# First V rows stored by the Pool queue, Wo issued right behind Wk, V rows of two segments loaded by the ACT queue, constants built first

## The chip, the cores and the metric

One core of a Trainium2 chip, bfloat16 data. The metric is the device time of one execution in microseconds (us); medians are of a kernel's runs. Engines: PE is the TensorE matmul, PEld its weight load, DVE VectorE, ACT ScalarE, POOL GpSimd, SP SyncE, which here only issues DMAs. All times "at x us" are counted from the first instruction of the profiled execution.

## The reference, cut to what matters

```python
def _A_ref(x, mem0, Wq, Wk, Wv, Wo, seg_len):     # x: 1 x 2048 x 512; 32 heads of 128; seg_len 32; 8 memory rows
    mem = mem0
    for s in range(64):
        h = concatenate([mem, x[:, 32*s : 32*s + 32]], axis=1)              # 40 rows
        q, k, v = (einsum('btd,dhe->bhte', h, W) for W in (Wq, Wk, Wv))
        p = softmax(where(mask, einsum('bhqe,bhke->bhqk', q, k) * scale, -1e9))
        o = einsum('bhte,hed->btd', einsum('bhqk,bhke->bhqe', p, v), Wo)
        mem = o[:, :8]                       # the next segment needs Wo of this one
        outs.append(o[:, 8:])
    return concatenate(outs, axis=1)
h  = x + _A_ref(layernorm(x), ...)
h2 = h + _B_ref(layernorm(h), ...)           # a gated MLP with a 2048 x 2048 spatial weight
```

The 64 segments form a chain: `mem` of one feeds the next, so no segment can start before the one ahead is through Wo.

## The kernel before

Wq, Wk, Wv and Wo stay in SBUF during the loop. Each is 4.19 MB and is loaded in four quarters of 1 MB. Before the loop the kernel computes the projections of the *extra rows* (8 rows of each segment) for the first "chunks" of 16 segments. V of such rows is scaled, written to DRAM (`vext_d`, eight stores of 128 KB for chunk 0, four for the first half of chunk 1) and read back in another layout as `Vx`, two loads of 32 KB for each segment.

```python
def vx_mm(ck, n, bank, only=None):                    # the matmuls are line L498 of the profile
    ...
def vx_evac(ck, n, bank, eng="act"):
    ...                                               # scale PSUM into t by ACT or DVE
    dst = vext_d[ck, n // 4, 2 * (n % 4):2 * (n % 4) + 2, :, :].rearrange("g p f -> p g f")
    sp(lambda e: e.dma_start(dst, t.rearrange("p (g f) -> p g f", g=2)), reads=tok, writes=[("vext", ck, n)])   # L514

def load_vx(s):
    i = s % CK
    for b in range(2):
        src = vext_d[s // CK, b, :, 8 * i:8 * i + 8, :].rearrange("g k (r e) -> g (k r) e", r=2)
        sp(lambda e, b=b, src=src: e.dma_start(Vx[:, s % NVX, b, :], src),                                       # L520
           reads=[("vext", s // CK, n) for n in range(4 * b, 4 * b + 4)], writes=[("Vx", s % NVX, b)])
```

The load phase, in program order. SP is one queue of instructions, and what stands behind a waiting one waits too: in the trace of this kernel SP reaches the first `Vx` load at 45.35 us, issues the second at 48.51, and issues the two quarters of Wo behind these loads at 50.39 and 50.89.

```python
for mi in (2, 1):                                     # Wv, then Wk (Wq was issued earlier)
    for hq in range(4):
        load_w(mi, hq)
def load_wo(hq):                                      # L822
    sp(lambda e, hq=hq: e.dma_start(w_o[:, 8 * hq:8 * hq + 8, :], wor[:, 8 * hq:8 * hq + 8, :]), writes=[("Wo", hq)])
    em.mark_const(("Wo", hq))
def start_group(mm, ev, *a):
    ...
    mm(*a, bk)
    ev(*a, bk, "act" if cnt % 2 == 0 else "dve")
def start_v(ck, n):
    start_group(vx_mm, vx_evac, ck, n)

for i in range(2, 8):                                 # Q of the extra rows
    for ck in range(2):
        start_group(qkx_mm, qkx_evac, ck, i)          # matmuls L463, evictions L473
    if i == 6:
        for j in range(4, 7):
            ln_stats(j)                               # row statistics, 2 of 4 steps by Pool
        late_consts()                                 # masks, ones, selectors: some 60 Pool instructions
for n in range(8):                                    # V of the extra rows, each followed by a store on SP
    ...
    start_v(0, n)
    if n % 2 == 1:
        start_v(1, n // 2)
    ...
    if n == 4:
        ...
        load_wo(0)
load_wo(1)
for j in range(2):
    load_vx(j)
for i in range(8, 16):                                # K of the extra rows, needs Wk
    start_group(qkx_mm, qkx_evac, 0, i)
    if i in (11, 13):
        load_wo(i // 2 - 3)
```

In a segment, PE runs the projections (L289, L290), S, PV (L664 with V, L670 with Vx; 666 and 672 after the change) and then Wo (L699; 701 after), with matmuls of later extra rows (L498) between.

```python
WOQ = ((0, 0), (2, 0), (0, 1), (2, 1), (1, 0), (3, 0), (1, 1), (3, 1))
def Wo(cbs, bank, d0, d1):
    for c, b in cbs:
        for g in range(4):
            h = 16 * b + 4 * c + g                    # quarter h // 8 of Wo
            pe(lambda e, ...: e.matmul(..., lhsT=cTh[:, i, 8:40], rhs=w_o[:, h, d0:d1], ...), reads=[("cT", c, b), ("Wo", h // 8)], ...)
```

Of the kernel before, what the change touches and what calls it, by code (L numbers as in the profile page):

```python
# [178 lines left out]
def fast_path(nc, st, keep, A_x, A_mem0, A_Wq, A_Wk, A_Wv, A_Wo, A_seg_len, B_w_in, B_w_sp, B_b_sp, B_w_out, out):  # L179
# [15 lines left out]
    CK = 16  # L195
# [9 lines left out]
    em = Emitter(n_dma_sems=40)  # L205

    def sb(name, shape, dt):
        return st.enter_context(nc.sbuf_tensor("f_" + name, shape, dt))
# [26 lines left out]
    NVX = 3  # L235
    Vx = sb("Vx", [128, NVX, 2, 128], BF)
# [41 lines left out]
    def PB(b):  # L278
        return ("ps", b)

    def sp(fn, **k):
        return em.add("sp", fn, dma=True, **k)

    def pe(fn, **k):
        return em.add("pe", fn, **k)
# [9 lines left out]
    def act(fn, **k):  # L295
        return em.add("act", fn, **k)

    def dve(fn, **k):
        return em.add("dve", fn, **k)

    def pool(fn, **k):
        return em.add("pool", fn, **k)
# [10 lines left out]
    def xbuf(j):  # L313
        return (xn[:, j, :], [("xn", j)]) if j < 2 else (part[:, j, :], [("part", j, 0), ("part", j, 1)])
# [33 lines left out]
    def late_consts():  # L348
        pool(lambda e: e.memset(ones[:], 0.0), writes=["ones"])
        pool(lambda e: e.memset(Sc[:], 0.0), writes=["Sc"])  # L350
        pool(lambda e: e.memset(mask[:], 0.0), writes=["mask"])
        for c in range(4):
            q = slice(32 * c, 32 * c + 32)
            pool(lambda e, q=q: e.memset(ones[q, q], 1.0), writes=["ones"])
            pool(lambda e, q=q: e.affine_select(out=G_sb[q, :], in_=onesrc[q, 0:M], pattern=[[-1, M]], compare_op=ALU.is_equal,
                                                fill=0.0, base=0, channel_multiplier=1), reads=["onesrc"], writes=["G"])
            pool(lambda e, q=q: e.affine_select(out=F_sb[q, :], in_=onesrc[q, 0:32], pattern=[[-1, 32]], compare_op=ALU.is_equal,
                                                fill=0.0, base=-M, channel_multiplier=1), reads=["onesrc"], writes=["F"])
            pool(lambda e, q=q: e.affine_select(
                out=Sc[q, :].rearrange("p (s r) -> p s r", r=32)[:, :, XM:32], in_=onesrc[q, 0:32].rearrange("p (s r) -> p s r", r=8),  # L360
                pattern=[[-8, 4], [-1, 8]], compare_op=ALU.is_equal, fill=0.0, base=0, channel_multiplier=1),
                reads=["onesrc"], writes=["Sc"])
            m1 = mask[q, 0:160].rearrange("p (g t) -> p g t", t=40)[:, :, 16:40]
            pool(lambda e, m1=m1: e.affine_select(out=m1, in_=m1, pattern=[[0, 4], [1, 24]], compare_op=ALU.is_ge,
                                                  fill=NEG, base=8, channel_multiplier=-1), reads=["mask"], writes=["mask"])
            pool(lambda e, q=q: e.memset(mask[q, 160:224], NEG), writes=["mask"])
            for k in range(8):
                m2 = mask[q, 160:224].rearrange("p (hp r t) -> p hp r t", hp=2, r=2)[:, :, :, k:16]
                pool(lambda e, m2=m2, k=k: e.affine_select(out=m2, in_=m2, pattern=[[-16, 2], [-1, 2], [0, 16 - k]],
                                                           compare_op=ALU.not_equal, fill=0.0, base=-2 * k, channel_multiplier=1),  # L370
                     reads=["mask"], writes=["mask"])
        pool(lambda e: e.tensor_copy(out=mask[:, 224:448], in_=mask[:, 0:224]), reads=["mask"], writes=["mask"])


    def ln_bn(j):
        t, tok = xbuf(j)
        k = j % 3
        dve(lambda e: e.bn_stats(out=st1[:, k, :], in_=t), reads=tok, writes=[("st1", k)])

    def ln_root(j):  # L380
        k = j % 3
        dve(lambda e: e.bn_aggr(out=mv1[:, k, :], in_=st1[:, k, :]), reads=[("st1", k)], writes=[("mv1", k)])
        act(lambda e: e.activation(out=rs1[:, k:k + 1], in_=mv1[:, k, 1:2], func=ACT.Ln, bias=EPS), reads=[("mv1", k)], writes=[("rs1", k)])
        act(lambda e: e.activation(out=rs1[:, k:k + 1], in_=rs1[:, k:k + 1], func=ACT.Exp, scale=-0.5), reads=[("rs1", k)], writes=[("rs1", k)])

    def ln_stats(j):
        k = j % 3
        ln_bn(j)
        dve(lambda e: e.bn_aggr(out=mv1[:, k, :], in_=st1[:, k, :]), reads=[("st1", k)], writes=[("mv1", k)])
        pool(lambda e: e.tensor_scalar(out=rs1[:, k:k + 1], in0=mv1[:, k, 1:2], scalar1=EPS, scalar2=None, op0=ALU.add),  # L390
             reads=[("mv1", k)], writes=[("rs1", k)])
        pool(lambda e: e.tensor_tensor(out=rs1[:, k:k + 1], in0=rs1[:, k:k + 1], in1=mhalf[:, 0:1], op=ALU.pow),
             reads=[("rs1", k), "mhalf"], writes=[("rs1", k)])

    def ln_apply(j):
        t, tok = xbuf(j)
        k = j % 3
        dve(lambda e: e.tensor_scalar(out=t, in0=t, scalar1=mv1[:, k, 0:1], scalar2=rs1[:, k:k + 1], op0=ALU.subtract, op1=ALU.mult),
            reads=tok + [("mv1", k), ("rs1", k)], writes=tok)
# [99 lines left out]
                                                       start=(dc == 0), stop=(dc == DC - 1), tile_position=(0, 32 * c)),  # L499
                   reads=[("hTe", ck % 3, dc // 2), ("W", 2, n // 2)], writes=[PB(bank)])  # L500

    def vx_evac(ck, n, bank, eng="act"):
        if ck == 1 and n < 4:
            t, tok = (hbuf, xo)[n // 2][:, n % 2, :], [(("h", "xo")[n // 2], n % 2)]
        elif ck == 0:
            t, tok = part[:, n, :], [("part", n, 0), ("part", n, 1)]
        else:
            t, tok = Vs[:, 0, :], [("Vs", 0)]
        if eng == "act":
            act(lambda e: e.activation(out=t, in_=ps[:, bank, :], func=ACT.Copy, scale=VSC), reads=[PB(bank)], writes=tok)  # L510
        else:
            dve(lambda e: e.tensor_scalar(out=t, in0=ps[:, bank, :], scalar1=VSC, scalar2=None, op0=ALU.mult), reads=[PB(bank)], writes=tok)
        dst = vext_d[ck, n // 4, 2 * (n % 4):2 * (n % 4) + 2, :, :].rearrange("g p f -> p g f")
        sp(lambda e: e.dma_start(dst, t.rearrange("p (g f) -> p g f", g=2)), reads=tok, writes=[("vext", ck, n)])  # L514

    def load_vx(s):
        i = s % CK
        for b in range(2):
            src = vext_d[s // CK, b, :, 8 * i:8 * i + 8, :].rearrange("g k (r e) -> g (k r) e", r=2)
            sp(lambda e, b=b, src=src: e.dma_start(Vx[:, s % NVX, b, :], src),  # L520
               reads=[("vext", s // CK, n) for n in range(4 * b, 4 * b + 4)], writes=[("Vx", s % NVX, b)])



# [270 lines left out]


    act(lambda e: e.preload_act_table_set("natural_log_exp_and_others"))
    for _ in range(44):
        pe(lambda e: e.matmul(ps[:, 1, 0:128], lhsT=onesrc[:, 0:128], rhs=onesrc[:, 0:128], start=True, stop=True), reads=["onesrc"], writes=[PB(1)])
    ln_bn(0)  # L800
# [20 lines left out]
# [3 lines that stand above are left out]
# [4 lines left out]
    def start_group(mm, ev, *a):  # L828
        cnt = scnt[0]
        scnt[0] += 1  # L830
        bk = ebank[cnt % 4]
        mm(*a, bk)
        ev(*a, bk, "act" if cnt % 2 == 0 else "dve")

    def start_v(ck, n):
        start_group(vx_mm, vx_evac, ck, n)

    for i in range(2, 8):
        for ck in range(2):
            start_group(qkx_mm, qkx_evac, ck, i)  # L840
        if i == 6:
            for j in range(4, 7):
                ln_stats(j)
            late_consts()
    for n in range(8):
        if n < 3:
            ln_apply(n + 4)
# [3 lines that stand above are left out]
        if n == 2:  # L851
            xT(4, 6)
            ring_copy(0, 6)
        if n == 3:
            xT(5, 7)
            ring_copy(1, 7)
        if n == 4:
            xT(6, 6)
            xe_copy(2, 6)
            mem0_transpose(7)  # L860
            load_wo(0)
    load_wo(1)
    for j in range(2):
        load_vx(j)
    for i in range(8, 16):
        start_group(qkx_mm, qkx_evac, 0, i)
        if i in (11, 13):
            load_wo(i // 2 - 3)


    gx = []
# [287 lines left out]
    for rb in range(RB):  # L1159
# [19 lines left out]
        if rb in (2, 3):  # L1179
            r, j, bank = RB - 4 + rb, (rb - 1) % 2, zbank()  # L1180
# [49 lines left out]
    for tb in range(NTB):  # L1230
        for fb in range(len(ACC) if tb == 0 else 0, FB):
            if tb == 0:
                bank = 5 + fb % 3
            else:
                bank = MB[mcnt % 3]
# [19 lines left out]
    for d0 in (0, 256):  # L1255
        bank = 7 if d0 else 5
# [766 lines left out]
```

## Time and profile before

| | before |
|---|---|
| median of 3 runs | 862.03 us (860.3 to 863.04) |
| profiled execution, granted clock | 860.6 us, 0.992 |
| segment 0 / 1 / 2 | 21.12 / 10.78 / 9.73 us |
| last quarter of Wk / of Wo landed | 40.35 / 60.34 us |

Start with the page: the busy shares, and the span in 40 slices of 21.5 us, where each digit is a tenth.

```profile
span 860.6 us, 45965 instructions
...
PE 837.9 (97%) x22497; PEld 440.7 (51%) x19432; DVE 513.7 (60%) x1318; ACT 471.1 (55%) x1361; POOL 165.2 (19%) x423
...
PE   8959999999999999999999999999999999999997
...
PEclk9979999999999999999999999999999999999999
...
GB/s 319 371 248 39 91 55 42 65 59 71 69 94 42 69 62 44 65 42 65 59 71 71 87 47 96 54 97 72 59 57 50 186 282 1 1 110 98 37 13 40
...
q8 instruction: 166, 2.72, 1.4%
...
PE 94%; DMA 2%; SPq 1%; DVE 1%; ACT 1%; issue 1%
```

PE is busy 97% of the span, so only a few per cent can be won at all. The digit that stands out is slice 3 (43 to 65 us): PE 5, its clock 7. The rest of the span is full. (The line for q8 is needed later: 2.72 MB in 166 packets is 16 KB each.)

The stretches of the first three segments, with busy time and number of instructions of each engine, the clock, the DMA share and the rate:

```profile
core 0: us, PE busy (x) PEld busy (x) DVE busy (x) ACT busy (x) POOL busy (x), PEclk, DMA share, GB/s
42.34:63.46 21.12, 12.09 (x318) 6.10 (x269) 6.28 (x17) 5.57 (x17) 3.33 (x10) 0.73 0.92 251
63.46:74.24 10.78, 10.53 (x321) 5.21 (x273) 6.70 (x19) 6.13 (x20) 2.48 (x6) 0.89 0.11 35
74.24:83.97 9.73, 9.48 (x321) 4.93 (x274) 6.24 (x18) 6.12 (x20) 1.69 (x4) 1.00 0.19 51
```

The same 320 matmuls take 9.73 us in segment 2, and 21.12 us in segment 0. So 11.39 + 1.05 = 12.4 us is all that this part can give. What PE waited for from 22 to 64 us (in total, number, longest):

```profile
PE f_ps L699 <- DMA f_arena<-in_A_Wo_dram: 6.9, 2, 3.7
PE f_ps L664 <- DMA f_Vx<-vext_d: 1.4, 2, 1.2
PE f_ps L498 <- issue: 0.7, 1, 0.7
PE f_ps L463 <- DMA f_arena<-in_A_Wk_dram: 0.6, 1, 0.6
```

Why is Wo late? The timeline of SP (start, duration, line, transfer, count):

```profile
18.07 9.15 SPq L329 DMA_DIRECT2D f_arena<-in_A_Wk_dram  x4
27.26 5.79 SPq L514 DMA_DIRECT2D vext_d<-f_part  x2
...
38.37 1.09 SPq L822 DMA_DIRECT2D f_arena<-in_A_Wo_dram  x1
...
44.28 0.89 SPq L822 DMA_DIRECT2D f_arena<-in_A_Wo_dram  x1
45.35 5.00 SPq L520 DMA_DIRECT2D f_Vx<-vext_d  x4
50.39 1.09 SPq L822 DMA_DIRECT2D f_arena<-in_A_Wo_dram  x2
```

Half of Wo is issued only at 50.39 us, because the four `Vx` loads ahead of it wait for stores that landed as late as 48.5 us. Meanwhile the DMA engines ran dry:

```profile
core 0: us, PE busy (x) PEld busy (x) DVE busy (x) ACT busy (x) POOL busy (x), PEclk, DMA share, GB/s
...
49.00:53.00 4.00, 1.90 (x52) 0.57 (x40) 1.41 (x6) 1.07 (x5) 1.23 (x3) 0.89 0.56 153
```

### The profile page before, as it was taken

What the parts mean: (1) busy time and instruction counts of PE and PEld (TensorE: products, weight loads), DVE (VectorE), ACT (ScalarE), POOL (GpSimd) and SP (SyncE); (2) the same over time, 40 slices, a digit from 0 to 9 for tenths busy, and PEclk for the clock granted to TensorE, in tenths of its full rate; (3) what the DMA queues carried; (4) which work ended last, traced back from release to release, by engine and by line L of the source; (5) the groups of instructions that cost most, each with busy time, mean ns of one, the idle gap of its engine ahead of it and who ended that gap; (6) DMA issues with size and microseconds to landing.
All of it is one profiled execution on the core that took longest, in us unless ns stands there. A gap on an engine that the chain in (4) does not pass through costs nothing.

```text
span 860.6 us, 45965 instructions
## 1 busy us (share of the span) xinstructions
PE 837.9 (97%) x22497; PEld 440.7 (51%) x19432; DVE 513.7 (60%) x1318; ACT 471.1 (55%) x1361; POOL 165.2 (19%) x423
## 2 busy tenths in 40 slices
PE   8959999999999999999999999999999999999997
PEld 8624555555555555555555555555555544444443
DVE  3436666666766666666766666666666564463443
ACT  3325676666666676666665666767666655400000
POOL 0712212221212112221212121122111232100000
PEclk9979999999999999999999999999999999999999
DMA  9991322222332222212222414243221690033101
GB/s 319 371 248 39 91 55 42 65 59 71 69 94 42 69 62 44 65 42 65 59 71 71 87 47 96 54 97 72 59 57 50 186 282 1 1 110 98 37 13 40
DMA packets 114714, 75.27 MB, mean 87 GB/s; under 512 B 70728, under 2 KB 100560, under 8 KB 114512
## 3 DMA queue, kind: packets, MB, share of 16 engines
q1 hardware_dynamic: 114224, 72.06, 30.7%
q8 instruction: 166, 2.72, 1.4%
q14 instruction: 36, 0.29, 0.1%
q10 hardware_dynamic: 288, 0.20, 0.1%
HBM read 39.46 MB, written 20.58 MB: 70 GB/s over the span
## 4 chain that ended last, share of the span: by engine, by line
PE 94%; DMA 2%; SPq 1%; DVE 1%; ACT 1%; issue 1%
PE f_ps L289 32%; PE f_ps L699 14%; PE f_ps L290 12%; PE f_ps L1138 11%; PE f_ps L498 3%; PE f_ps L749 3%; PE f_ps L664 3%; PE f_ps L1212 3%; PE f_ps L1100 3%; PE f_ps L1131 3%; PE f_ps L463 2%; PE f_ps L593 1%; PE f_ps L613 1%; DMA f_arena<-in_A_Wo_dram 1%; PE f_ps L670 1%; PE f_ps L720 1%
## 5 line engine op out<-in xcount | busy, mean ns | idle before, releaser
L289 PE MATMUL f_ps<-f_arena,f_hT 128*32 128x512 bf16 (+1 forms) x5632 | 361.0, 332 | 0.2
L289 PEld LDWEIGHTS f_ps<-f_arena,f_hT 128*32 128x32 bf16 x5632 | 134.7, 96 | 160.9 <-issue 69.5
L290 PE MATMUL f_ps<-f_arena,f_hT 128*32 128x512 bf16 (+1 forms) x2560 | 190.1, 316 | 0.0
L557 ACT ACTIVATE f_Tst<-f_ps 128x512 bf16<-128x512 f32 (+1 forms) x320 | 149.7, 510 | 57.7 <-PE f_ps L289 54.0
L699 PE MATMUL f_ps<-f_arena,f_cT 128*32 128x256 bf16 x4096 | 133.2, 276 | 8.5 <-DMA f_arena<-in_A_Wo_dram 6.9
L636 POOL TENSOR_TENSOR f_E_sb<-f_R_sb,f_E_sb 128x64 bf16<-128x64 f32 x128 | 56.9, 445 | 353.1 <-ACT f_R_sb L628 353.1
L699 PEld LDWEIGHTS f_ps<-f_arena,f_cT 128*32 128x32 bf16 x4096 | 90.8, 95 | 45.8 <-ACT f_cT L684 23.9
L565 DVE STREAM_TRANSPOSE f_QT<-f_Tst 128x256 uint32<-128x256 uint32 x128 | 57.1, 446 | 95.0 <-ACT f_Tst L557 95.0
L1138 PE MATMUL f_ps<-f_arena 128*128 128x512 bf16 x448 | 100.6, 379 | 0.0
L686 DVE TENSOR_SCALAR f_cT<-f_ps 128x160 bf16<-128x160 f32 x256 | 65.2, 317 | 37.0 <-PE f_ps L670 37.0
L711 ACT ACTIVATE f_part<-f_ps 128x256 bf16<-128x256 f32 x128 | 49.0, 383 | 66.5 <-PE f_ps L699 62.4
L656 DVE TENSOR_SCALAR f_V_sb<-f_ps 128x512 bf16<-128x512 f32 (+1 forms) x128 | 71.0, 555 | 13.7 <-PE f_ps L289 13.7
L684 ACT ACTIVATE f_cT<-f_ps 128x160 bf16<-128x160 f32 x256 | 57.1, 310 | 38.1 <-PE f_ps L670 38.1
L1138 PEld LDWEIGHTS f_ps<-f_arena 128*128 128x128 bf16 x448 | 43.7, 98 | 52.8
L565 DVE STREAM_TRANSPOSE f_KT<-f_Tst 128x128 uint32<-128x128 uint32 (+1 forms) x192 | 66.0, 356 | 2.7
L624 ACT ACTIVATE f_R_sb<-f_ps 128x160 f32<-128x160 f32 x128 | 38.9, 304 | 35.0 <-PE f_ps L290 35.0
L632 DVE TENSOR_TENSOR f_E_sb<-f_R_sb,f_E_sb 128x160 bf16<-128x160 f32 x128 | 41.7, 326 | 23.3 <-ACT f_R_sb L628 23.3
L1144 DVE TENSOR_TENSOR f_arena<-f_ps,f_arena 128x512 f32<-128x512 f32 x28 | 19.3, 690 | 54.4 <-PE f_ps L1138 52.4
L289 PE MATMUL f_ps<-f_arena,f_hTe 128*32 128x512 bf16 x640 | 48.9, 382 | 0.0
L606 ACT ACTIVATE f_E_sb<-f_ps 128x224 bf16<-128x224 f32 x128 | 45.9, 359 | 0.0
L749 PE MATMUL f_ps<-f_arena,f_cTx 128*32 128x512 bf16 x512 | 44.0, 379 | 0.0
L628 ACT ACTIVATE f_R_sb<-f_R_sb 128x160 f32<-128x160 f32 x128 | 42.6, 332 | 2.0
(116 smaller groups left out, 1021.8 us busy)
## 6 DMA issues: line engine op xcount, KB each, us to landing
wT_d<-f_wst SPq DMA_DIRECT2D x32, 256.0 KB
f_arena<-wT_d SPq DMA_DIRECT2D x32, 256.0 KB
f_arena<-in_A_Wv_dram SPq DMA_DIRECT2D x4, 1024.0 KB
f_arena<-in_A_Wk_dram SPq DMA_DIRECT2D x4, 1024.0 KB
f_arena<-in_A_Wo_dram SPq DMA_DIRECT2D x4, 1024.0 KB
f_Vx<-vext_d SPq DMA_DIRECT2D x128, 32.0 KB
f_arena<-in_A_Wq_dram SPq DMA_DIRECT2D x3, 1024.0 KB
vext_d<-f_Vs SPq DMA_DIRECT2D x20, 128.0 KB
```

The source lines that it names most:

```text
L289: return e.matmul(out, lhsT=lhsT, rhs=rhs, start=start, stop=stop, skip_group_check=True, tile_position=pos)
L290: return e.add_instruction(mybir.InstMatmult(name=nc.get_next_instruction_name(), engine=mybir.EngineType.PE, ins=[e.lower_ap(rhs), e.lowe ...
L557: act(lambda e: e.activation(out=st_.rearrange("p (hp i r) -> p hp i r", i=32, r=2), in_=ps[:, bank, 0:64 * np_].rearrange("p (hp r i) -> ...
L565: dve(lambda e: e.transpose(out=dst, in_=src), reads=tok, writes=[(nm, b, k) for k in halves(b, p0, np_)])
L636: pool(lambda e: e.tensor_tensor(out=ev, in0=rv, in1=ev, op=ALU.mult), reads=[("R", b), ("Ex", b)], writes=[("Ex", b)])
L656: dve(lambda e: e.tensor_scalar(out=dst, in0=src, scalar1=VSC, scalar2=None, op0=ALU.mult), reads=[PB(bank)], writes=tok)
L684: act(lambda e: e.activation(out=dst, in_=src, func=ACT.Copy, scale=UNSC), reads=[PB(PVB[c])], writes=tok)
L686: dve(lambda e: e.tensor_scalar(out=dst, in0=src, scalar1=UNSC, scalar2=None, op0=ALU.mult), reads=[PB(PVB[c])], writes=tok)
L699: pe(lambda e, h=h, g=g, i=i, b=b, c=c: e.matmul(ps[32 * g:32 * g + 32, bank, 0:d1 - d0], lhsT=cTh[:, i, 8:40], rhs=w_o[:, h, d0:d1], star ...
L711: act(lambda e: e.activation(out=part[:, s % 8, d0:d1], in_=ps[:, bank, 0:d1 - d0], func=ACT.Copy), reads=[PB(bank)], writes=[("part", s % ...
L749: pe(lambda e, h=h, g=g, i=8 * qr + bg: e.matmul(ps[32 * g:32 * g + 32, WXB, :], lhsT=cTx[:, rb % 2, i, :], rhs=w_o[:, h, :], start=(i < 4 ...
L1138: pe(lambda e: e.matmul(ps[:, bank, 0:TB], lhsT=z2[:, sc, fb * 128:(fb + 1) * 128], rhs=wTb[tb % 2][:, :, sc, :], start=(sc == 0), stop=(s ...
```

## The change

The intent is that no transfer PE needs soon should be issued behind one that has to wait. Wo goes right behind Wk. The eight stores of chunk 0 go to Pool's queue, the four of chunk 1 behind everything, and the first four `Vx` loads to ACT's queue. Pool must be free by then, so the constants are built at the very start, and three row statistics move from Pool to ACT.

```diff
-    def vx_evac(ck, n, bank, eng="act"):
+    def vx_evac(ck, n, bank, eng="act", q="sp"):
...
-        sp(lambda e: e.dma_start(dst, t.rearrange("p (g f) -> p g f", g=2)), reads=tok, writes=[("vext", ck, n)])
-
-    def load_vx(s):
+        if q is not None:
+            em.add(q, lambda e: e.dma_start(dst, t.rearrange("p (g f) -> p g f", g=2)), reads=tok, writes=[("vext", ck, n)], dma=True)
+        return lambda: sp(lambda e: e.dma_start(dst, t.rearrange("p (g f) -> p g f", g=2)), reads=tok, writes=[("vext", ck, n)])
+
+    def load_vx(s, q="sp"):
...
+            em.add(q, lambda e, b=b, src=src: e.dma_start(Vx[:, s % NVX, b, :], src), ..., dma=True)
...
     act(lambda e: e.preload_act_table_set("natural_log_exp_and_others"))
+    late_consts()
...
     def start_v(ck, n):
-        start_group(vx_mm, vx_evac, ck, n)
+        if ck == 0:
+            start_group(vx_mm, lambda *a: vx_evac(*a, q="pool"), ck, n)
+        else:
+            stores.append(start_group(vx_mm, lambda *a: vx_evac(*a, q=None), ck, n))
...
             for j in range(4, 7):
-                ln_stats(j)
-            late_consts()
+                ln_bn(j)
+                ln_root(j)
...
-            load_wo(0)
-    load_wo(1)
-    for j in range(2):
-        load_vx(j)
+    for hq in range(4):
+        load_wo(hq)
     for i in range(8, 16):
         start_group(qkx_mm, qkx_evac, 0, i)
-        if i in (11, 13):
-            load_wo(i // 2 - 3)
+    for j in range(2):
+        load_vx(j, "act")
+    for f in stores:
+        f()
```

More of the change, by code (lines that the diff above doesn't have):

```diff
@@ L519, in load_vx @@
             src = vext_d[s // CK, b, :, 8 * i:8 * i + 8, :].rearrange("g k (r e) -> g (k r) e", r=2)
-            sp(lambda e, b=b, src=src: e.dma_start(Vx[:, s % NVX, b, :], src),
-               reads=[("vext", s // CK, n) for n in range(4 * b, 4 * b + 4)], writes=[("Vx", s % NVX, b)])
+            em.add(q, lambda e, b=b, src=src: e.dma_start(Vx[:, s % NVX, b, :], src),
+                   reads=[("vext", s // CK, n) for n in range(4 * b, 4 * b + 4)], writes=[("Vx", s % NVX, b)], dma=True)
     QKP = ((0, 0, 8, 0, 0), (0, 0, 8, 1, 1), (1, 0, 8, 0, 6), (1, 0, 4, 1, 7), (1, 4, 4, 1, 2))
@@ L832, in start_group @@
         mm(*a, bk)
-        ev(*a, bk, "act" if cnt % 2 == 0 else "dve")
+        return ev(*a, bk, "act" if cnt % 2 == 0 else "dve")
+    stores = []
     def start_v(ck, n):
-        start_group(vx_mm, vx_evac, ck, n)
+        if ck == 0:
+            start_group(vx_mm, lambda *a: vx_evac(*a, q="pool"), ck, n)
+        else:
+            stores.append(start_group(vx_mm, lambda *a: vx_evac(*a, q=None), ck, n))
     for i in range(2, 8):
```

## The prediction

Wo's landing came to 60.4 - 2.4 - 1.8 - 0.8 = 55.4 us, and the gain to 5.0 (60.4 to 55.4) + 2.4 (1.4 + 1.0, for the clock) = 7.4 us, from 862.03 to about 854.7. Of these terms the 0.8 us names no trace. That the shorter wait spares the clock (the 2.4 us), and that the stores beside Wk cost it their full 3.6 us, were my estimates.

> **What bounds the kernel now.** The page of the profile gives PE 97% busy and 94% of the chain of waits; the rest lies almost wholly in the start. The PE timeline shows a steady segment of 9.73 us (74.24 to 83.97 us). Segment 0 takes 21.1 us (42.34 to 63.46), segment 1 takes 10.8. So about 12.4 us is lost there. Inside segment 0 PE waits 1.4 us for V rows (Vx) and 6.9 us for Wo; the fourth quarter of Wo lands at 60.4 us. The stretch table shows the granted clock at 0.5 from 53 to 65 us. [...]
>
> Why Wo is late: the SP issue list shows two quarters of Wo only at 50.4 us, behind stores and four Vx loads that wait for those stores (last store landed 48.5). DMA moves 360 to 390 GB/s up to 40 us; from 49 to 53 it falls to 80 to 260 GB/s.
>
> **What the change does.**
> - Wo is issued right behind Wk, from about 27 us, so the ring never runs dry. The gap of 49 to 53 us (about 0.9 MB, my estimate 2.4 us) goes.
> - The four stores of the second V chunk (0.5 MB, about 1.8 us at the 290 GB/s that I work out for the stores) go behind Wo. The w_sp transpose no longer overlaps Wo's last quarter (about 0.8 us).
> - The eight stores of the first chunk move to the Pool queue, beside Wk. [...] 1.05 MB of stores (about 3.6 us) now delay Wk. PE should wait for Wk about 3 us more before segment 0 (before: 1.1 us in all).
> - Vx is loaded early by ACT: PE's 1.4 us wait for Vx goes. ACT pays four issues (about 0.6 us each on SP) just ahead of its first evictions.
> - Constants move to an idle Pool's first 20 us; three row statistics move to ACT (0.2 us per activation). Neither is on the chain.
>
> **Sum.** Wo's last quarter lands near 60.4 - 2.4 - 1.8 - 0.8 = 55.4 us. PE reaches Wo near 53.6 (Wk-late start of segment 0 at 46, plus 7.6), so it still waits about 2 us: DMA bandwidth, not issue order, is then the limit. The shorter wait keeps the clock at 1.0, which saves about 1.4 us in Wo of segment 0 and 1.0 us in segment 1. Gain: 5.0 + 2.4 = 7.4 us.
>
> Predicted 854.7 us (-0.85%), range 851.0 to 859.0. Faster by over 2%: 0.02; within 2%: 0.96; slower by over 2%: 0.02.
>
> **What would show it right.** Segment 1 starts near 57.5 us instead of 63.5; clock 1.0 throughout; DMA above 300 GB/s up to 55 us without a gap; no wait for Vx; a wait for Wo of 1 to 3 us; waits for Wk of 3 to 5 us; segment 1 near 9.7 us.
>
> **What would make it wrong.** Pool's stores get a small share of the engines: Wk is then earlier but Vx later, and ACT, which waits for the stores, holds up its evictions. [...] If stores overlap loads at little cost, Wo lands near 52.5 and the gain is 10 us.

## The result, and the profile after

| | before (same rounds) | after |
|---|---|---|
| median of 4 runs | 861.25 us (860.3 to 863.04) | 855.64 us (855.21 to 855.9) |
| ratio of fast runs | | 0.9932, 95% interval 0.9913 to 0.9951 |
| profiled execution, granted clock | 860.6 us, 0.992 | 854.1 us, 0.998 |
| segment 0 / 1 | 21.12 / 10.78 us | 14.10 / 10.21 us |
| last quarter of Wk / of Wo landed | 40.35 / 60.34 us | 42.20 / 55.21 us |

A ratio here is the mean time of one kernel's fast runs over the mean of the other's in the same rounds, so it is not quite the ratio of the medians that are quoted. The change is faster by 0.7%, which is inside the 2% that count as the same, and its interval excludes 1.

The page after:

```profile
span 854.1 us, 45974 instructions
...
PE 837.4 (98%) x22504; PEld 442.0 (52%) x19432; DVE 513.3 (60%) x1318; ACT 472.5 (55%) x1367; POOL 169.1 (20%) x425
...
PE   8889999999999999999999999999999999999997
...
PE 92%; SPq 3%; DMA 2%; DVE 1%; ACT 1%; issue 1%; ACTq 0%
```

PE's busy time has hardly moved (837.9 to 837.4 us). The gain is idle time of PE alone: the digit 5 of slice 3 is an 8, while slice 2 went from 9 to 8, since Wk now comes later. The three segments and PE's waits (22 to 64 us):

```profile
core 0: us, PE busy (x) PEld busy (x) DVE busy (x) ACT busy (x) POOL busy (x), PEclk, DMA share, GB/s
44.20:58.30 14.10, 11.07 (x318) 6.25 (x268) 6.09 (x17) 5.45 (x17) 1.69 (x4) 0.92 0.90 273
58.30:68.51 10.21, 9.96 (x321) 5.10 (x272) 6.70 (x19) 6.14 (x20) 2.49 (x6) 0.94 0.26 74
68.51:78.24 9.73, 9.47 (x321) 4.90 (x274) 6.23 (x18) 6.13 (x20) 1.69 (x4) 1.00 0.20 52
```

```profile
PE f_ps L498 <- issue: 2.6, 1, 2.6
PE f_ps L463 <- DMA f_arena<-in_A_Wk_dram: 1.6, 2, 1.4
PE f_ps L498 <- ACT f_arena L473: 0.7, 1, 0.7
```

Segment 0 starts 1.86 us later, since the stores now run beside Wk, and segment 1 starts 5.16 us earlier (63.46 to 58.30). Segment 1 itself is 0.57 us shorter. The other 0.8 us of the 6.5 us between the two profiled spans comes from later: the sum of segments 3 to 62 is 588.16 and 587.77 us, what follows (segment 63 and the part behind the loop) 188.47 and 188.06. Segments 3 to 62 differ by 5.3 us between the changed kernel and wo_held below (587.77 and 593.10 us), which are the same there. Sporadic PE waits of up to 0.7 us for which the profile names no releaser go with it: from 70 to 670 us they add up to 0.8 us in the changed kernel, 1.2 in the kernel before and 3.9 in wo_held. So a part of a small difference in time is such jitter, and I compare the start of segment 1 as well as the time. What these waits are comes out of experiments 9 and 10.

The waits for Wo and for `Vx` are gone by name, and a new one of 2.55 us stands there, which the profile calls "issue": it found nothing that released it. Where it lies, in PE's timeline:

```profile
52.03 0.61 PE L498 MATMUL f_ps<-f_arena,f_hTe 128*32 128x512 bf16 x7
55.19 0.38 PE L498 MATMUL f_ps<-f_arena,f_hTe 128*32 128x512 bf16 x1 [2.55 <-issue]
55.20 1.71 PE L701 MATMUL f_ps<-f_arena,f_cT 128*32 128x256 bf16 x39
```

It ends at 55.19 us, and the last quarter of Wo landed at 55.21. The obvious reading is a wait for Wo with the name missing. But that matmul doesn't read Wo. What it is became the main question of the experiments. The issue lists of SP and of Pool show the change at work:

```profile
17.11 11.23 SPq L329 DMA_DIRECT2D f_arena<-in_A_Wk_dram  x4
28.39 16.81 SPq L825 DMA_DIRECT2D f_arena<-in_A_Wo_dram  x4
45.25 3.66 SPq L516 DMA_DIRECT2D vext_d<-f_hbuf  x2
```

```profile
25.45 1.69 POOL L515 DMA_DIRECT2D vext_d<-f_part  x2 [5.09 <-ACT f_part L510]
...
32.32 1.45 POOL L515 DMA_DIRECT2D vext_d<-f_part  x2 [2.67 <-DMA vext_d<-f_part]
```

SP takes 16.81 us for four issues of Wo, while the DMA engines move 387 GB/s, and is done with them at 45.20 us, 10.0 us before the last of Wo lands. The first packet of Pool's first store starts at 29.79 us, 4.3 us after its issue. Pool's stores land from 31.79 to 40.56 us, some 6 us after their issue, and Pool waits 2.67 us for an older store before it issues the fifth. ACT spends 3.11 us on its four issues of `Vx` (43.55 to 46.66), just ahead of its first evictions of segment 0.

### The profile page after: what moved, and what is told of

The parts are those of the page before. It is cut to its first block, busy times and chain, and to the rows that moved or that the text cites. A ratio compares the mean times of both kernels' runs of the same rounds, so it can differ in the third digit from the quotient of the medians.

```text
span 854.1 us, 45974 instructions
## 1 busy us (share of the span) xinstructions
PE 837.4 (98%) x22504; PEld 442.0 (52%) x19432; DVE 513.3 (60%) x1318; ACT 472.5 (55%) x1367; POOL 169.1 (20%) x425
## 4 chain that ended last, share of the span: by engine, by line
PE 92%; SPq 3%; DMA 2%; DVE 1%; ACT 1%; issue 1%; ACTq 0%
PE f_ps L289 33%; PE f_ps L701 14%; PE f_ps L290 12%; PE f_ps L1146 11%; PE f_ps L751 3%; PE f_ps L666 3%; PE f_ps L1220 3%; PE f_ps L1108 3%; PE f_ps L1139 3%; SPq L329 2%; PE f_ps L498 2%; DMA f_arena<-in_A_Wk_dram 2%; PE f_ps L595 1%; PE f_ps L615 1%; PE f_ps L672 1%
```

## The experiments

The rivals:

- **A**, the prediction's own: bytes and their order in the load stream set when Wo and `Vx` land, and the landing of Wo ends segment 0, whichever queue issues the stores.
- **B**: issuing Wo early is the whole gain, and the other parts are decoration.
- **C**: the wait without a name is not for Wo.
- **D**: the stores must leave SP, because SP waits there for each eviction and then issues Wo late.

Twelve kernels ran. The median of the kernel before was 862.45 us (the first four kernels below), 858.85 (the next four) and 861.22 (the last four).

### 1. Only Wo moved (wo_early_only)

```diff
 # against before
         load_w(mi, hq)
+    for hq in range(4):
+        load_wo(hq)
...
-            load_wo(0)
-    load_wo(1)
...
-        if i in (11, 13):
-            load_wo(i // 2 - 3)
```

> The kernel before with one part of the change: Wo issued right behind Wk; the twelve V stores and the four Vx loads stay on SP, so they now queue behind Wo. Theory A (the gain needs Wo early and the V path off SP[...]): Wo lands near 52 us and PE no longer waits for it, but the last V store lands near 57 and Vx near 59, PE waits for Vx some 8 to 10 us at half clock after it, segment 1 starts at 62 to 65 us (before 63.5): 860 to 863 us, no gain. Rival B (Wo's place in the SP queue is by itself what the change gains): 855 to 857 us.

Measured: 861.66 us, ratio 0.9986 (0.9974 to 0.9998). Wo landed at 42.95, 45.89, 48.90 and 52.65 us, 7.7 us earlier than before, and it brought hardly anything. PE's waits:

```profile
PE f_ps L664 <- DMA f_Vx<-vext_d: 9.1, 2, 7.4
```

The V stores and `Vx` now queue behind Wo on SP (the last `Vx` load is issued at 58 us), so a 9.1 us wait for `Vx` takes the place of the 6.9 us wait for Wo. B falls. Moving one transfer ahead only moves the wait to what was pushed back.

### 2. Half of Wo held back (wo_held)

```diff
 # against after
-    for hq in range(4):
+    for hq in range(2):
         load_wo(hq)
...
+        if s == 0:
+            for hq in (2, 3):
+                load_wo(hq, [em.by_eng["act"][-1]])      # behind an ACT instruction of segment 0
```

> The changed kernel with Wo's quarters 2 and 3 held back until V of segment 0 is evicted (near 51.6 us); all else as changed. Theory A (Wo's landing sets the end of segment 0): Wo lands near 58 us instead of 55.2, PE's wait is long enough to halve the clock, segment 1 starts near 61 to 62 us: 858 to 860 us. Rival C (PE's 2.6 us wait at 52.6 us is a late fetch of PE's own instructions, since the wait ends at 55.19 before Wo's landing at 55.21, and the freed SP and V path are what gained): within 1 us of the changed kernel, 855 to 856.5 us.

Measured: 866.49 us, ratio 1.0043 (1.0028 to 1.0058), above what either expected. The two quarters were issued from 53.15 us on, landed at 59.90 and 62.72, and PE waited for Wo:

```profile
PE f_ps L701 <- DMA f_arena<-in_A_Wo_dram: 7.9, 2, 5.5
```

Segment 1 started at 65.84 instead of the expected 61 to 62, 7.5 us after the changed kernel's. Wo landed 7.5 us later as well, so a late Wo is paid in full. The profiled run, the slowest of the six, is worse than that alone explains by some 5 us, which lies in segments 3 to 62 (593.10 us against 587.77); some 3 us of it are more of the sporadic waits without a name. In sign this is A's; both sizes were missed.

### 3. The stores back on SP, everything else as changed (stores_sp)

```diff
-            start_group(vx_mm, lambda *a: vx_evac(*a, q="pool"), ck, n)
+            start_group(vx_mm, lambda *a: vx_evac(*a, q="sp"), ck, n)
```

> The changed kernel with the first chunk's eight V stores back on SP, ahead of Wo there; Vx loads stay on ACT, the second chunk's stores stay behind Wo. Theory A (bytes in the ring are the limit, whichever queue issues them): Wk's last quarter lands near 40.4 us instead of 42.2, segment 0 starts near 42.4, Wo still lands at 54.5 to 56, segment 1 starts at 57.5 to 59: 855 to 856.5 us, the same as changed within 0.1%. Rival D (stores must leave SP, because SP waits there for each eviction and then issues Wo late): Wo lands at 57 or later, 858 to 860 us.

Measured: 860.13 us, ratio 0.9974 (0.9962 to 0.9987). A missed, and D's numbers were right. SP's timeline:

```profile
28.07 12.18 SPq L515 DMA_DIRECT2D vext_d<-f_part  x8
40.29 6.87 SPq L825 DMA_DIRECT2D f_arena<-in_A_Wo_dram  x4
```

The last quarter of Wk landed at 41.14 us, 1.2 us earlier than in the next kernel (42.32). The last quarter of Wo landed at 57.72, against 55.21 and 55.25 in the two traces of the changed kernel (and 54.24 in the next kernel, where the `Vx` loads, too, run behind Wo). So the same bytes in one queue cost Wo about 2.5 us, and A's sentence "whichever queue issues" is false.

Wo is issued late, as D says, but hardly because SP waits for evictions: the last of the eight ended at 35.11 us, and SP issued the last store at 39.17. The eight issues took SP 12.18 us. So it issues Wo's first quarter only at 40.29 us, and the DMA engines, which had moved 379 GB/s from 30 to 40 us, moved 188 GB/s from 40 to 42 and 163 from 42 to 44. That is 0.70 MB in 4 us; at the 335 GB/s of this run from 43 to 56 us it would have taken 2.1, so an estimated 1.9 us were lost. The rest is rate: from 30 to 40 us the changed kernel moved 399 GB/s, 5% more (its Pool stores went out in packets of 4,096 bytes, SP's here in 512; whether that is why is not shown). In series, the last store landed 2.94 us after Wk; beside it, the stores delayed Wk by 1.2 us, and by 1.9 from before to after. So stores beside loads are partly free.

### 4. Vx loaded by SP, everything else as changed (vx_sp)

```diff
-        load_vx(j, "act")
+        load_vx(j)
```

> The changed kernel with the Vx loads of segments 0 and 1 back on SP, so behind Wo. Theory A[...]: Vx lands at 55.5 to 56.5 us, PE waits for it from 51.2 us on, the clock halves, segment 1 starts at 60.5 to 62 us: 858 to 860 us. If loading Vx by ACT is not needed: 855 to 856 us. ACT loses no time to issues any more, so S of segment 0 starts 0.3 us earlier in any case.

Measured: 857.69 us, ratio 0.9947 (0.9927 to 0.9967). `Vx` of segment 0 landed at 53.98 and 54.16 us, some 1.5 us ahead of A's range. PE waited for it,

```profile
PE f_ps L666 <- DMA f_Vx<-vext_d: 3.0, 1, 3.0
```

and then for nothing else: Wo had landed at 54.24. Segment 1 started at 58.40 us, against 58.30 in the changed kernel. Both times were missed (858 to 860 with A, 855 to 856 if the loads by ACT are not needed). Loading `Vx` by ACT removes the wait for `Vx`, as predicted, but it is worth nothing by itself, because another wait ends at the same time.

### 5. The changed kernel once more (changed_again)

Not edited.

> The changed kernel unedited, on the same chip as the next three, for comparison: 0.993 of the kernel before, segment 1 starts near 58.3 us, segment 2 near 68.5. PE's wait near 52.6 us ends near 55.2 us, within 0.1 us of Wo's last quarter, if both causes coincide by chance the two times will differ by more on this chip.

Measured: 855.25 us, ratio 0.9956 (0.9938 to 0.9974). So the gain is 0.4 to 0.7%. The wait without a name is there again, at the same matmul:

```profile
55.07 0.38 PE L498 MATMUL f_ps<-f_arena,f_hTe 128*32 128x512 bf16 x1 [1.12 <-issue]
```

It was 1.12 us and ended at 55.07 us, 0.18 us *before* the last quarter of Wo landed (55.25). A wait for that quarter cannot end before it lands, so it is not that wait.

### 6. A wrong result: no last quarter of Wo at all (wo3_zero)

```diff
-    for hq in range(4):
+    for hq in range(3):
         load_wo(hq)
+    pool(lambda e: e.memset(w_o[:, 24:32, :], 0.0), writes=[("Wo", 3)])
+    em.mark_const(("Wo", 3))
```

> The changed kernel with Wo's last quarter set to zero by Pool instead of loaded (a wrong result, on purpose): 1 MB less in the ring before Wo is complete. Theory A (PE's 2.6 us wait at 52.6 us is Wo's landing): Wo's third quarter lands near 51.2 us as before, so PE starts Wo at 52.7 us without a wait, the clock stays at 1.0, segment 1 starts at 54.7 to 55.2 us and segment 2 at 64.5: 851.5 to 853 us. Rival C (the wait is a late fetch of PE's instructions, which the profile marks as no releaser): PE still waits 1 to 2.5 us at the same instruction, with no DMA of Wo outstanding; segment 1 starts at 56 to 57.5 us.

Measured: 853.03 us, ratio 0.9937 (0.9915 to 0.9959). Segment 0 took 10.39 us and segment 1 started at 56.06, later than A expected only because segment 0 started late here (45.68 us; PE had waited 1.95 us for Wk, and the clock was at half from 40.87 to 44.28). The nameless wait was gone, so C's expectation was missed. That looks like a proof of A, but the run took away two things at once: with 1 MB less to load, the packet of PE's instructions that experiments 9 and 10 turn on also came early (51.04 to 52.04 us, against 52.62 to 53.82, although segment 0 had started 1.5 us later). What the run does bound: with neither cause segment 0 is 0.66 us over a steady segment and 3.7 us under the changed kernel's, of which 2.2 us show in the start of segment 1 here.

### 7. The constants built late again (consts_late)

```diff
-    late_consts()
...
-                ln_bn(j)
-                ln_root(j)
+                ln_stats(j)
+            late_consts()
```

> The changed kernel with the constants and the three row statistics put back as before the change (Pool: statistics at 22 to 25 us, then constants to 44 us). Theory A (constants first is what lets Pool issue the V stores in time; off the chain otherwise): Pool issues the eight stores only from 44 us, the last lands near 55 us, ACT stands still before the Vx loads until then and with it the evictions of segment 0; segment 1 starts at 66 to 69 us: 863 to 867 us. If the order of the constants doesn't matter: 855 to 856.5 us.

Measured: 865.71 us, ratio 1.0085 (1.0064 to 1.0106), as expected. PE's waits:

```profile
PE f_ps L580 <- POOL f_QT L574: 7.1, 1, 7.1
PE f_ps L595 <- DVE f_KT L567: 6.0, 1, 6.0
```

Pool issues the V stores only at 44.19 to 53.6 us, behind the constants; ACT, which must wait for them before it issues `Vx`, makes its first eviction of segment 0 at 59.06 us. Building the constants first is not decoration: without it, stores on Pool lose 0.85% instead of winning. (The run moves the three statistics back as well; experiment 11 shows that these alone change nothing.)

### 8. An attempt at a better kernel (best1)

`Vx` of segment 0 is issued by SP between the second and third quarter of Wo, and in segment 0 the heads of Wo's last quarter are multiplied last.

```diff
-    for hq in range(4):
+    for hq in range(2):
+        load_wo(hq)
+    load_vx(0)
+    for hq in range(2, 4):
         load_wo(hq)
...
-    for j in range(2):
-        load_vx(j, "act")
+    load_vx(1)
...
+        if s == 0:                      # (2, 1) and (3, 1), the last quarter's heads, come last
+            Wo(WOF[:6], OB, 0, OC)
+            Wo(WOF[:6], OB2, OC, D)
+            Wo(WOF[6:], OB, 0, OC)
...
```

> A version meant to beat both: the changed kernel with Vx of segment 0 issued on SP between Wo's second and third quarter (so not as 256-byte packets beside Wo, and ACT freed of four issues), Vx of segment 1 behind Wo, and in segment 0 alone the heads of Wo's last quarter taken last, for both halves of the columns. Theory A (Wo's landing at 54 to 55 us is the limit): only 16 of 64 Wo matmuls remain after it, segment 1 starts at 55.5 to 56.5 us, segment 2 at 65.3 to 66.3: 853 to 854.5 us, 2 us under the changed kernel. Rival C (instruction fetch is the limit): PE starts Wo no earlier than 55.2 us, segment 1 at 57.5 to 58 us, within 0.7 us of the changed kernel.

Measured: 854.66 us, ratio 0.9954 (0.9936 to 0.9972), a tie with the changed kernel in the same call (0.9956). Of the two, C had the wait right (PE started Wo at 55.14 us); for the start of segment 1 both missed, as it came at 59.39 in the profiled run, the slowest of the six, with the clock at half from 55.5 us. PE had all that it needed by 52.22 us (`Vx` and three quarters of Wo; the last, which landed at 55.01, was 48 Wo matmuls away), and it still waited:

```profile
52.51 0.61 PE L498 MATMUL f_ps<-f_arena,f_hTe 128*32 128x512 bf16 x7
55.14 0.38 PE L498 MATMUL f_ps<-f_arena,f_hTe 128*32 128x512 bf16 x1 [2.02 <-issue]
```

So the wait is not for Wo's last quarter. In the nine traces listed under the next two runs it falls after exactly 1729 PE instructions (1727 matmuls and weight loads, and two others at the start), although the kernels differ in what PE waits for before. And each time it ends 1.3 to 1.5 us after a 16 KB packet of the queue that the page lists as "q8 instruction". That led to the next two runs.

### 9 and 10. Shift the instruction count (shift_minus, shift_plus)

If PE waits for its instructions, the wait belongs to a *count* of instructions. If it waits for a semaphore, it belongs to a *place* in the program. Eight warm-up matmuls less take 16 PE instructions away ahead of segment 0; ten tiny matmuls more, put into a wait for Wk, add 20.

```diff
 # shift_minus, against after
-    for _ in range(44):
+    for _ in range(36):
         pe(lambda e: e.matmul(ps[:, 1, 0:128], lhsT=onesrc[:, 0:128], rhs=onesrc[:, 0:128], ...
```

```diff
 # shift_plus, against after
     for i in range(8, 16):
+        if i == 14:
+            for _ in range(10):
+                pe(lambda e: e.matmul(ps[:, 1, 0:8], lhsT=onesrc[:, 0:128], rhs=onesrc[:, 0:8], ...
         start_group(qkx_mm, qkx_evac, 0, i)
```

> The changed kernel with 36 instead of 44 warm-up matmuls, that is 16 fewer TensorE instructions ahead of segment 0 and nothing else. Instruction-fetch theory: TensorE's wait without a releaser in segment 0 stays at TensorE instruction no. 1729, which is now about 8 Wo matmuls further into the program than the last L498 matmul (no. 1713), and it ends 1.3 to 1.5 us after the end of a 16,384-byte packet of the instruction queue. Rival, a wait that belongs to a point of the program (a semaphore that the profile failed to name, such as Wo's last quarter): the wait stays at the last L498 matmul, now instruction no. 1713. Time 854 to 857 us with either.

> The changed kernel with ten tiny dummy matmuls (128x8) put into TensorE's wait for Wk, 20 more TensorE instructions ahead of the same place. Instruction-fetch theory: the wait without a releaser moves back in the program, to instruction no. 1729, 20 instructions ahead of the last L498 matmul (now about no. 1749), in the last PV or first L498 matmuls, and ends 1.3 to 1.5 us after the end of the packet; the evictions that follow come after it, so 0.3 to 1 us longer. Rival, a point of the program: it stays at the last L498 matmul (no. 1749), and the time is within 0.2% of the changed kernel's.

Measured: 857.0 us, ratio 0.9957 (0.9939 to 0.9974), and 857.17 us, ratio 0.9958 (0.9941 to 0.9975). PE's timeline of the kernel with 16 fewer instructions:

```profile
53.02 0.61 PE L498 MATMUL f_ps<-f_arena,f_hTe 128*32 128x512 bf16 x8
53.47 0.40 PE L701 MATMUL f_ps<-f_arena,f_cT 128*32 128x256 bf16 x7
54.87 1.64 PE L701 MATMUL f_ps<-f_arena,f_cT 128*32 128x256 bf16 x49 [1.00 <-issue]
```

and of the one with 20 more:

```profile
51.89 0.20 PE L672 MATMUL f_ps<-f_E_sb,f_Vx 32*128 32x64 bf16 x1
54.91 0.21 PE L672 MATMUL f_ps<-f_E_sb,f_Vx 32*128 32x64 bf16 x3 [2.82 <-issue]
55.05 0.62 PE L498 MATMUL f_ps<-f_arena,f_hTe 128*32 128x512 bf16 x8
```

With 16 fewer, the wait moved 8 matmuls on: one L498 and seven of Wo. With 20 more, it moved ten matmuls back: seven of L498 and three of PV. Both are exact, and both stand after 1729 PE instructions again. A wait for a place of the program is excluded. My list of the packets of q8, from the traces:

```
kernel            packet (us)       PE stops after   PE goes on at   after the packet's end
before            49.80 to 50.91    1729             52.25           1.34
after             52.62 to 53.82    1729             55.19           1.37
changed_again     52.51 to 53.57    1729             55.07           1.50
best1             52.59 to 53.74    1729             55.14           1.40
stores_sp         51.66 to 52.87    1729             54.22           1.35
shift_minus       52.40 to 53.46    1729             54.87           1.41
shift_plus        52.38 to 53.58    1729             54.91           1.33
stats_pool        52.12 to 53.18    1729             54.61           1.43
all_stores_pool   53.34 to 54.42    1729             55.86           1.44
```

So the wait is PE's own supply of instructions: shown is that it follows the count, and that it ends a constant 1.3 to 1.5 us behind the packet.

The other waits without a name in the traces of the kernel before and of the changed kernel fit. From 20 us on these two have seven PE waits of over 0.2 us for which the profile names no releaser. They fall after 1729, 12,737, 27,329 and 32,961 PE instructions in the kernel before and after 1729, 9,665 and 33,473 in the changed one, each 193 more than a multiple of 256 (1729 is 6 x 256 + 193), and they end 1.2 to 1.5 us behind a packet of q8. The page fits as well: 166 packets for 41,929 matmuls and weight loads are one for 253. So what was called jitter above is, in these two traces, the same supply.

Why the packet is late stays open. Counted from PE's instruction 1473, which is 256 earlier, it starts 3.7 us later in the kernel before (46.14 to 49.80 us) and 4.1 us later in the changed kernel (48.54 to 52.62). In the changed kernel the DMA engines moved 323 to 331 GB/s from 49 to 52 us; whether that delays the packet is not shown. The traces don't show when a packet was asked for.

No run removes this wait and leaves all else. In shift_minus the last quarter of Wo landed at 54.98 us, 0.11 us after the wait ended, and it is read from the 13th Wo matmul on, so without the wait PE would soon have stood before Wo. The two limits coincide.

### 11. The row statistics back on Pool (stats_pool)

```diff
-                ln_bn(j)
-                ln_root(j)
+                ln_stats(j)
```

> The changed kernel with the three row statistics back on the Pool engine (constants still built first, V stores after them). If the 0.66 us that TensorE waits for ACT at 24 us counted, the time falls by about 0.6 us; my theory is that Wk's last quarter sets the start of segment 0, so that the wait for Wk grows by what the wait for ACT loses, and the ratio is within 0.3% of the changed kernel's 0.993 to 0.996.

Measured: 857.47 us, ratio 0.996 (0.9944 to 0.9976), level with the two kernels above. The 0.7 us wait for ACT is gone from PE's list, and the wait for Wk is 2.9 us instead of 1.6. Segment 0 started at 45.20 us, not earlier. Wk itself landed 1.0 us later in this trace (43.21 us): segment 0 started 1.99 us after Wk's last quarter here and 2.00 us after it in the changed kernel, so Wk sets its start and the wait for ACT doesn't count. That agrees with the prediction, which had the statistics off the chain.

### 12. All twelve stores by Pool (all_stores_pool)

The four stores of chunk 1 no longer follow Wo.

```diff
-        if ck == 0:
-            start_group(vx_mm, lambda *a: vx_evac(*a, q="pool"), ck, n)
-        else:
-            stores.append(start_group(vx_mm, lambda *a: vx_evac(*a, q=None), ck, n))
+        start_group(vx_mm, lambda *a: vx_evac(*a, q="pool"), ck, n)
```

> The changed kernel with all twelve V stores issued by Pool ahead of or beside the weights, so the last four no longer follow Wo. Theory: the four stores (0.5 MB) are bytes ahead of Wo: Wo's last quarter lands 1 to 2 us later (56 to 57.5 us) and segment 1 starts 0.8 to 2 us later than the 58.3 us of the changed kernel; time +0.5 to +1.5 us, 855.5 to 857.5 us. Rival, stores beside loads are nearly free (as the stores by Pool against stores by SP suggest): Wo's last quarter within 0.5 us of 55.2, time within 0.4 us.

Measured: 857.83 us, ratio 0.9967 (0.9949 to 0.9986). Wo's last quarter landed at 55.79 us, which hits neither number: A wanted 56 or more, the rival 55.7 or less. Wk had landed 0.76 us later than in the changed kernel (42.96 to 42.20), so from Wk to the end of Wo it is 12.83 us, against 13.01 without these stores in between. Segment 1 started at 58.09 us. The intervals of all four kernels overlap. So the four stores beside Wo cost less than 1 us and probably about nothing, and the 1.8 us that the prediction gave them is not supported.

## Why the prediction was right or wrong

Predicted 854.7 us; measured 855.64. The time, the direction and the mechanism (the late Wo, hidden behind stores and `Vx` loads on SP) were right. The gain was to be 7.4 us and was 5.6 by the medians (6.5 between the profiled executions), and the sum hides errors that cancelled, so the close hit is partly luck. Of the parts of the change, stores on Pool's queue and constants first were needed (0.9974 and 1.0085 without them). `Vx` by ACT, the four stores behind Wo and the statistics on ACT could each be taken back alone for 0.9947 to 0.9967, against 0.9932 and 0.9956 with all; they were not taken back together.

- **"Wo's last quarter lands near 55.4."** Measured 55.21. The terms were wrong in opposite directions. Stores beside Wk were to cost "about 3.6 us"; Wk came 1.85 us later (40.35 to 42.20). With 3.6 us Wk would have ended at 43.95 and Wo 11.4 us behind it; Wo took 13.0 us. The mis-sized term is the cost of the stores: I took bytes over a rate, from stores that ran in series, and stores_sp shows that in series and beside are not the same (2.94 against 1.2 us). The 0.8 us for the w_sp transpose was not tested.
- **"The four stores of the second chunk (about 1.8 us) go behind Wo."** Done, but all_stores_pool finds no such cost beside Wo.
- **"The gap of 49 to 53 us goes."** Right: 320 GB/s from 49 to 55 us in the changed kernel, where the kernel before had 153 from 49 to 53.
- **"PE's 1.4 us wait for Vx goes."** Right, and worth nothing by itself: in vx_sp the wait is 3.0 us and segment 1 starts 0.1 us later.
- **"PE waits for Wk about 3 us more."** Too large, for the same reason as the first term: 1.57 us in all, plus 0.66 us for ACT, whose removal brought nothing in stats_pool. Segment 0 started at 44.20, not 46.
- **"It still waits about 2 us: DMA bandwidth is then the limit."** The size was right (2.55 us), the cause half right. Wo's last quarter landed at 55.21 us and PE's wait for its instructions ended at 55.19. best1 took the first away and won nothing; shift_minus moved the second and won nothing, and no run removes the second alone.
- **"The shorter wait keeps the clock at 1.0", 1.4 + 1.0 us.** This step failed in the profiled run. The clock fell to half from 56.05 us for 3.41 us, where before it was half for 13.65 us from 52.12. That the shorter wait would spare the clock was my estimate; no trace of this case gave a length of wait for it, and two sentences about one are cut from the prediction. The trace before: there the clock fell ahead of the two long waits for Wo, when PE had been idle for 1.97 of the last 3.41 us. In the changed kernel a single wait of 2.55 us was enough, in best1 one of 2.0 us, in stats_pool two of 0.9 us within 2.4 us, and in changed_again one of 1.12 us was not. No run tests what separates these cases. What the traces of the kernel before and of the changed kernel show: from its first record to the drop at the end, each stretch of one clock is a whole multiple of 3.41 us long (47.79, 13.65 and 795.3; 51.20, 3.41 and 795.3). Cut into steps of 3.41 us from that first record (to 80 us), the clock fell after the steps in which PE was idle for 1.97 us (before) and 2.55 us (after), by the profile's modelled ends of matmuls, and stayed full after all others, with at most 1.49 and 1.36 us. At half it stayed after steps with 2.61, 3.01 and 1.44 us idle (before) and rose after one with none (both). From the end of the wait to segment 1 it took 3.11 us (55.19 to 58.30) against 2.24 (55.07 to 57.31) in changed_again, and segment 1 took 10.21 against 9.72: about 1.4 us of the predicted 2.4 us didn't come in this execution. The later part of the program made up for some of it, so the total came out near all the same; in other executions it seems to fall for longer or not at all (their mean clocks run from 0.996 to 1.0, and 3.4 us at half are 0.002 of the span).
- **"Constants move to an idle Pool; neither is on the chain."** Right for where they went, but what they leave behind was on it: consts_late is 1.3% slower than the changed kernel of its call (1.0085 to 0.9956).
- **Segment 1 "near 57.5".** Measured 58.30, of which the clock made some 0.9 us (3.11 against 2.24). "Segment 1 near 9.7 us": 10.21, the clock again.

## What to carry to other kernels

A transfer that must wait can hold up what is issued behind it on the same engine (here half of Wo, issued at 50.39 us behind `Vx` loads that SP had reached at 45.35); move the waiting ones to another queue, and then look at what was pushed back, since a single move (Wo early alone) only renamed the wait (9.1 us for `Vx` in place of 6.9 for Wo). Where several waits end within a microsecond of each other, removing one can gain nothing (without the wait for Wo's last quarter best1 came to 0.9954, against 0.9956 for the changed kernel in its call), so before improving on it find out by experiment which of them are there. A PE wait without a releaser may be its own instruction supply, as it was here: change the number of instructions ahead of it and see whether the wait moves with the count (16 fewer moved it 8 matmuls on, 20 more 10 back).
